# A three-stage kernel (top-k attention, a dense layer pair, routed experts): fixed engines for the weight splits of experts 2 to 7, and a new order of all operations

## The chip, the cores and the metric

One Trainium2 chip, one core of it. The metric is the device time of one execution in microseconds (us). The kernel before: median 687.64 us of 3 runs, 686.29 to 690.04.

## The reference

Three computations in a row, all in float32:

```
scores = q @ k^T / 8                      # 2 batches x 8 heads, 576 x 576, head size 64
keep the 32 largest of each row; softmax over them; attn @ v
x = attention output as 1152 tokens x 512
h = x @ w_in (512 x 2048);  x = (h * cos(h)) @ w_out (2048 x 512)
expert = argmax(x @ w_gate) of 8;  gate = its softmax weight
token t goes to slot "count so far" of its expert (capacity 288, later ones dropped)
out[t] = gate * relu(x @ w1[expert] (512 x 1024)) @ w2[expert] (1024 x 512)
```

## The kernel before, in words

**Engines.** TensorE (PE) does matmuls and transposes, VectorE (DVE), ScalarE (ACT) and GpSimd (POOL) the elementwise work, SyncE (SP) issues the loads. Each has its own queue and works through it in order.

**First stage (attention, dense pair, routing).** The 16 heads are worked in 36 steps of 128 query rows for two heads. A step: `scores` (L716, PE) and their eviction to `Sp`; `pair_chain` (L751, DVE), which finds the 32nd largest value of each row with repeated maximum and replace instructions; `softmax` (L791, ACT, POOL, DVE); `products` (L826), transposes and the product with `v`. When the steps of a tile of 128 tokens are done, `layer_in`, `cosine`, `product` and `layer_out` (L911 to L986) do the dense pair, `route` and `place` (L988, L1026) choose the expert and scatter the token rows to `xs` in DRAM. Meanwhile `convert` (L605) turns the dense weights, which arrive as 64-bit numbers, into float32.

**Expert stage.** For each of 8 experts: `gather` (L1204) loads up to 192 token rows `xg`, PE transposes them (`xp`, L1219 and L1220), ACT rounds the result into `xgs` (L1222) and DVE subtracts to get the rest (L1223). `expert_in` (L1226) multiplies with `w1` (`hp`, L1234 and L1236), ACT copies (`ht`, L1239), DVE adds (L1240), ACT applies relu and rounds (`hc`, L1241), DVE makes the rest of `hc` in two instructions (`rest`, L1244, L1247). `expert_out` (L1252) multiplies with `w2` (`yp`, L1266), ACT scales by the gate (`ot`), and POOL scatters the rows to the output (L1272). After the main path a branch handles experts with over 192 tokens.

**Weight splits.** PE multiplies a rounded part and a rest of each weight. `weights2` (L1187) loads an expert's weights in 8 pieces of 512 KB into the `raw` buffers and splits each half-piece: `rounded` (L593) makes `wh` or `wk`, on ACT (L594) or POOL (L595); `subtract` (L589) makes the rest `wl`, on DVE (L590) or POOL (L591). There are 16 of each per expert. Two sets of split weights exist, so that the splits of an expert can run while the one before it computes; a set is free again once the expert two before it has used it.

**The order.** Nothing is ordered by hand. Each operation is handed to a planner (`Plan`, L276) with an engine, a cost in us and a rank. `emit` (L340) is a list scheduler: on each engine it takes, among the operations that could start within 0.02 us of the earliest, the one with the lowest rank, and writes the instructions in that order. `RANKS` holds a rank for every operation; `flex` (L330) lets one character of `PICKS` choose the engine of an operation that can run on two or three. An operation marked `port=True` waits in the plan for the other of DVE and POOL to end its marked one (L374). `tb` is the rank penalty of an ACT operation that needs another function table than the loaded one. `PICKS` is read in program order: 9 characters for each of the 36 steps, 32 for `convert`, 140 for the dense pair, then 32 for each expert.

Of the kernel before, what the change touches and what calls it, by code (L numbers as in the profile page):

```python
# [45 lines left out]
    "0000000000000000000000000000000000000000000000001000000010000000100000000000000000000000000000000000"  # L46
    "0000000000000000000000000000000000000000000000000000000000000000000000000000000000000000000000000000"
    "0001000000000000000000000000100011001100000001122000001122000001020011000000111110000110100011000100"
    "0220000001220110011020000000000000000000001011000000000000000000000001010000000010100001000000000101"
    "0101010101000000000000001110101101010110000000101010101010101010001010111010101101011111111111110000"  # L50
    "0000000101010101000000000000001000101010010000000000000100111110001000000000010111010000000101010111"
    "0000000000010100000101010000011000010101010100000011110101010000000000000000011110101000001000101000"
    "0001010101000000000010010101010101000100000010110000")
RANKS = [
# [431 lines left out]
def forward(ctx, lasting, tc, kq, vn, vs_, w_in, w_out, w_gate, w1, w2, out, paired):  # L486
# [172 lines left out]
    def hi_of(idx):  # L659
        return ("wk" if idx[0] > 1 else "wh", (idx[0], idx[1] // 2), idx[1] % 2)  # L660
# [90 lines left out]
    def pair_chain(s):  # L751
# [8 lines left out]
        for r in range(3):  # L760
            for i in range(2):
                P.op("dve", 0.365, lambda r=r, i=i: DVE.max(T["W", s][:, i, LIST[r]:LIST[r] + 8], T["C", s][:, i, 0:HS]),  # L762
                     r=[("C", s, i)], w=[("W", s, i)])
# [629 lines left out]
```

## Time and profile before

| what | us |
|---|---|
| median of 3 runs (lowest to highest) | 687.64 (686.29 to 690.04) |
| the profiled execution | 687.24 |
| its span, first to last instruction | 685.4 |
| PE, DVE, ACT, POOL busy | 595.2, 549.7, 468.1, 345.7 |
| loads, stores | 64.57 MB, 12.69 MB |

Times in rows are us from the start of the span unless marked ns. PE is a matmul, PEld a weight load, L12 a line of the kernel. A row of the groups view reads: line, engine, operation, output<-inputs with shapes, xcount | busy us, mean ns of one | idle time of the engine just before them and who ended it. In a timeline: start, length, instruction, xcount, and in brackets the engine's idle time before it and who ended that. Matmuls are pipelined and their ends are modelled. The granted clock is a share of 2.4 GHz.

### The profile page before, as it was taken

The numbers are of one execution on the slowest core, as the hardware profiler recorded it, in microseconds if no ns is written. First come the engines' busy times: TensorE is split into PE (matmuls) and PEld (weight loads), VectorE is DVE, ScalarE is ACT, GpSimd is POOL, SyncE is SP. The second block draws the span as 40 slices with busy tenths as digits, with TensorE's granted clock in tenths as the row PEclk, the third lists the DMA queues.
The fourth block names the chain that finished last, engine by engine and source line by source line (L and its number), as shares of the span: only waits on it lengthen the run. The fifth ranks groups of instructions, "written<-read, shape, count | busy, mean of one in ns | idle before, by whom it ended". The sixth has DMA issues, their size and how long they took to land.

```text
span 685.4 us, 11005 instructions
## 1 busy us (share of the span) xinstructions
PE 595.2 (87%) x3675; PEld 440.6 (64%) x3675; DVE 549.7 (80%) x1470; ACT 468.1 (68%) x954; POOL 345.7 (50%) x396
## 2 busy tenths in 40 slices
PE   2456896999999998999999999998597977989894
PEld 1134673676866556776667767764486856978793
DVE  5999999999999998999999935664367787758860
ACT  3689799999999996886758844734255555546541
POOL 1387887566598653523646525122135546623631
PEclk9997798999999998999999999999698999999997
DMA  8553359200411111000000023443435545644710
GB/s 341 216 203 123 122 202 343 91 32 1 143 47 48 55 40 35 2 0 1 1 2 1 1 78 121 140 139 138 155 112 186 202 159 195 235 150 149 233 48 18
DMA packets 30787, 77.29 MB, mean 113 GB/s; under 512 B 4606, under 2 KB 4606, under 8 KB 30720
## 3 DMA queue, kind: packets, MB, share of 16 engines
q1 hardware_dynamic: 28976, 71.73, 30.4%
q0 software_dynamic: 1744, 4.76, 1.8%
q8 instruction: 31, 0.51, 0.3%
q14 instruction: 36, 0.29, 0.1%
HBM read 64.57 MB, written 12.69 MB: 113 GB/s over the span
## 4 chain that ended last, share of the span: by engine, by line
PE 55%; DVE 18%; ACT 15%; issue 5%; DMA 3%; POOL 2%; SPq 1%; POOLq 0%; DVEq 0%; ACTq 0%
PE x L982 15%; PE yp L1266 8%; DVE hc L1247 5%; PE h L928 4%; PE av L851 4%; PE S L729 4%; PE pt L837 4%; PE h L933 3%; PE h L934 3%; PE h L935 3%; PE hp L1234 3%; DVE C L765 2%; DVE W L762 2%; ACT pen L803 2%; ACT Sp L820 2%
## 5 line engine op out<-in xcount | busy, mean ns | idle before, releaser
L982 PE MATMUL x<-wo,hs 128*128 128x512 f32 x288 | 139.9, 609 | 1.4 <-POOL hs L972 1.3
L807 POOL TENSOR_TENSOR Sp<-Sp,pen 128x576 f32<-128x576 f32 x59 | 80.7, 1367 | 38.4 <-ACT pen L803 35.5
L765 DVE MATCH_REPLACE8 C<-W,C 128x288 f32<-128x288 f32 x216 | 94.1, 442 | 0.0
L762 DVE MAX8 W<-C 128x8 f32<-128x288 f32 x216 | 90.8, 448 | 0.6
L729 PE MATMUL S<-kq 64*128 64x288 f32 x256 | 57.4, 530 | 28.0 <-ACT Sp L599 17.6
L1234 PE MATMUL hp<-xgs,wh 128*128 128x384 f32 x256 | 78.6, 373 | 0.0
L982 PEld LDWEIGHTS x<-wo,hs 128*128 128x128 f32 x288 | 49.7, 193 | 43.3 <-issue 39.9
L1266 PE MATMUL yp<-wk,hc 128*128 128x512 f32 x192 | 71.2, 419 | 0.0
L837 PE MATMUL pt<-ident,Sp 128*128 128x128 f32 x324 | 56.0, 302 | 11.4 <-ACT Sp L820 9.9
L837 PEld LDWEIGHTS pt<-ident,Sp 128*128 128x128 f32 x324 | 40.8, 154 | 38.8 <-ACT Sp L820 17.3
L1236 PE MATMUL hp<-xgs,wl 128*128 128x192 f32 x256 | 65.6, 256 | 0.0
L757 DVE TENSOR_TENSOR C<-Sp 128x576 f32<-128x576 f32 x72 | 61.2, 851 | 4.1 <-ACT Sp L599 3.1
L803 ACT ACTIVATE pen<-Sp,tb 128x576 bf16<-128x576 f32 x72 | 55.5, 771 | 7.2 <-POOL tb L796 4.4
L810 ACT ACTIVATE Sp<-Sp,tb 128x576 f32<-128x576 f32 x72 | 55.8, 776 | 4.0 <-DVE Sp L807 2.4
L1247 DVE SCALAR_TENSOR_TENSOR hc<-ht,hc 128x128 fp32r<-128x128 f32 (+1 forms) x128 | 53.8, 476 | 5.2 <-ACT hc L1241 4.4
L729 PEld LDWEIGHTS S<-kq 64*128 64x128 f32 x256 | 22.3, 213 | 50.3 <-ACT Sp L599 31.2
L935 PE MATMUL h<-xh,wl 128*128 128x256 f32 x192 | 53.8, 280 | 0.0
L853 PE MATMUL av<-PT,v 128*64 128x128 f32 x320 | 47.8, 301 | 5.8 <-ACT PT L599 5.8
L769 DVE MAX8 W<-C 128x8 f32<-128x576 f32 x72 | 52.3, 748 | 0.2
L1266 PE MATMUL yp<-wl,hc 128*128 128x512 f32 x128 | 52.5, 410 | 0.0
L599 ACT ACTIVATE PT<-pt 128x384 f32<-128x384 f32 x97 | 44.3, 486 | 11.1 <-PE pt L837 11.1
L591 POOL TENSOR_TENSOR wl<-raw,wk 128x512 fp32r<-128x512 f32 x26 | 34.1, 1330 | 35.2 <-ACT wk L594 32.3
(158 smaller groups left out, 1572.9 us busy)
## 6 DMA issues: line engine op xcount, KB each, us to landing
raw<-in_w_dram SPq DMA_DIRECT2D x64, 512.0 KB
wraw<-in_w_in_dram SPq DMA_DIRECT2D x16, 512.0 KB
wraw<-in_w_out_dram SPq DMA_DIRECT2D x16, 512.0 KB
xs<-z SPq DMA_DIRECT2D x1, 4680.0 KB
kq<-in_kq_dram SPq DMA_DIRECT2D x8, 576.0 KB
v<-in_vn_dram SPq DMA_DIRECT2D x8, 320.0 KB
v<-in_vs_dram SPq DMA_DIRECT2D x8, 320.0 KB
out_dram<-z SPq DMA_DIRECT2D x1, 2304.0 KB
```

The source lines that it names most:

```text
L729: PE.matmul(T[kp][:, a, 0:HS], t[p, 1, j * 128:(j + 1) * 128], t[p, 0, i * HS:(i + 1) * HS], start=True, stop=True)
L762: P.op("dve", 0.365, lambda r=r, i=i: DVE.max(T["W", s][:, i, LIST[r]:LIST[r] + 8], T["C", s][:, i, 0:HS]), r=[("C", s, i)], w=[("W", s, i)])
L765: P.op("dve", 0.42, lambda r=r, i=i: DVE.match_replace(T["C", s][:, i, 0:HS], T["W", s][:, i, LIST[r]:LIST[r] + 8], T["C", s][:, i, 0:HS], ...
L803: P.op("act", 0.67, lambda i=i, kp=kp: ACT.activation(T[kp], T["Sp", s][:, i, :], AF.Relu, scale=-BIG, bias=T["tb", s][:, i, 0:1]), r=[ks, ...
L807: eng.tensor_tensor(out=T["Sp", s][:, i, :], in0=T["Sp", s][:, i, :], in1=T[kp], op=OP.subtract)
L837: PE.transpose(T[kp][:, c * 128:(c + 1) * 128], P2[:, cc * 128:(cc + 1) * 128], ident)
L935: PE.matmul(o, lo, a, start=False, stop=(kc == 3), skip_group_check=True)
L982: P.op("pe", 0.86, lambda f=f, a=a: PE.matmul(T["x2", t], T[kh][:, a:a + 128], T["wo", 0][:, f, :], start=(f == 0), stop=(f == 15)), r=[kh ...
L1234: PE.matmul(T[kp][:, 0:2 * MAIN], hi_at(ka)[:, c:c + 128], x.rearrange("p a n -> p (a n)"), start=(kc == 0), stop=False, skip_group_check= ...
L1236: PE.matmul(T[kp][:, 0:MAIN], T[kb][:, c:c + 128], x[:, 0], start=False, stop=(kc == 3), skip_group_check=True)
L1247: DVE.scalar_tensor_tensor(h[:, d:d + c1 - c0], t[:, c0:c1], 0.0, h[:, c0:c1], op0=OP.max, op1=OP.subtract)
L1266: PE.matmul(T[kp], x, w, start=(fc + n == 0), stop=(fc == 7 and n == len(uses) - 1))
```

## The change

From the third expert on (`e > 1`) the splits no longer go through `flex`: every rounding is an ACT operation and every subtraction a DVE operation with `port=True`; `PICKS` shrinks from 752 to 560 characters. `rest` gets `port=True`. A number of costs change, most of them of PE. `tb` goes from 28.19 to 41.13, and all of `RANKS` and `PICKS` are new.

```diff
 PICKS = (
-    "0000000000000000000000000000000000000000000000001000000010000000100000000000000000000000000000000000"
...
+    "0000000000000000000010000000000000000000000000001000000010000000100000100000000010000000000000000000"
...
 RANKS = [
-    13.82, 76.33, 33.9, 115.9, -5.32, -4.16, 45.32, 21.36, 15.26, -3.5, -3.67, -3.5, -3.66, -0.54, -0.54, 0, 0, 0.7,
...
+    -57.65, -11.09, -55.03, 90.68, -38.73, -35.96, -6.67, 16.37, 16.37, -2.88, -4.35, -2.88, -4.35, -0.42, -0.42,
...
-PRM = dict(... tb=28.19, ...)
+PRM = dict(... tb=41.13, ...)
...
-        P.op("pe", 0.5 if kind == "n" else 1.0, mm, r=[k], w=[kp], ...)
+        P.op("pe", 0.595 if kind == "n" else 1.025, mm, r=[k], w=[kp], ...)
...
-                P.op("dve", 0.365, lambda r=r, i=i: DVE.max(T["W", s]...
+                P.op("dve", 0.372, lambda r=r, i=i: DVE.max(T["W", s]...
...
-        P.op("pool", 0.3, scalars, r=both + [("halfpi",)], w=[("edge", s), ("tb", s)])
+        P.op("pool", 0.5, scalars, r=both + [("halfpi",)], w=[("edge", s), ("tb", s)])
...
-            P.op("pe", 0.33, tr, r=parts + [CONST], w=[kp], duty=0.5)
+            P.op("pe", 0.345, tr, r=parts + [CONST], w=[kp], duty=0.5)
...
-        P.op("pe", 1.12 if kind == "n" else 2.2, av, ...
+        P.op("pe", 1.16 if kind == "n" else 2.24, av, ...
...
-                P.op("pe", 0.86, mm, r=xs_ + [("ws", w) for w in ws], w=[kp])
+                P.op("pe", 0.9, mm, r=xs_ + [("ws", w) for w in ws], w=[kp])
...
-                P.op("pe", 1.43, mm, r=xs_ + ...
+                P.op("pe", 1.46, mm, r=xs_ + ...
...
-            P.op("pe", 0.86, lambda f=f, a=a: PE.matmul(T["x2", t], ...
+            P.op("pe", 0.87, lambda f=f, a=a: PE.matmul(T["x2", t], ...
...
+    def T_part(k, a):
+        return lambda: T[k][:, a * 512:(a + 1) * 512]
+
     def weights2(e, i):
...
         for a in range(2):
             hi, lo = wkey("wh", e, i, a), wkey("wl", e, i, a)
-            rounded(lambda a=a, hi=hi: (hi_at(hi), T[kr][:, a * 512:(a + 1) * 512]), r=[kr], w=[hi])
-            subtract(lambda a=a, hi=hi, lo=lo: dict(out=T[lo], in0=T[kr][:, a * 512:(a + 1) * 512], in1=hi_at(hi)),
-                     r=[kr, hi], w=[lo])
+            part = T_part(kr, a)
+            if e > 1:
+                P.op("act", 0.52, lambda hi=hi, part=part: ACT.activation(hi_at(hi), part(), AF.Copy), r=[kr], w=[hi])
+                P.op("dve", 0.6, lambda hi=hi, lo=lo, part=part: DVE.tensor_tensor(
+                    out=T[lo], in0=part(), in1=hi_at(hi), op=OP.subtract), r=[kr, hi], w=[lo], port=True)
+                continue
+            rounded(lambda hi=hi, part=part: (hi_at(hi), part()), r=[kr], w=[hi])
+            subtract(lambda hi=hi, lo=lo, part=part: dict(out=T[lo], in0=part(), in1=hi_at(hi)), r=[kr, hi], w=[lo])
...
-        P.op("dve", 0.33, rest, r=[kt], w=[kc_])
+        P.op("dve", 0.335, rest, r=[kt], w=[kc_], port=True)
```

What the two strings of `PICKS` choose, counted by the operations in program order (number of operations on each engine, before and after):

| operation | before | after |
|---|---|---|
| scores evicted to `Sp`, steps 0 to 35 | ACT 67, DVE 5 | ACT 60, DVE 12 |
| penalty subtracted in `softmax` (L807) | POOL 59, DVE 13 | POOL 52, DVE 20 |
| scaling in `softmax` (L820 to L822) | ACT 59, DVE 3, POOL 10 | ACT 59, DVE 9, POOL 4 |
| transposes evicted to `PT` | ACT 97, DVE 11 | ACT 86, DVE 22 |
| `convert`, first operation | ACT 29, POOL 3 | ACT 26, POOL 6 |
| `layer_in`: eviction; clamp | ACT 15, DVE 21; POOL 23, DVE 13 | ACT 21, DVE 15; POOL 34, DVE 2 |
| `product` | POOL 23, DVE 13 | POOL 29, DVE 7 |
| `split_w`: rounding; subtraction | ACT 16; DVE 9, POOL 7 | ACT 14, POOL 2; DVE 6, POOL 10 |
| experts 0 and 1: rounding; subtraction | ACT 27, POOL 5; DVE 24, POOL 8 | ACT 19, POOL 13; DVE 18, POOL 14 |
| experts 2 to 7: rounding; subtraction | ACT 78, POOL 18; DVE 56, POOL 40 | ACT 96; DVE 96 (fixed) |

Nearly all of the changed picks of the steps lie in steps 19 to 35.

## Rows read from the trace of the kernel before

**Rows 1.** Windows: stretch, length; busy PE, PEld, DVE, ACT, POOL; clock; DMA share, GB/s
```profile
60.00:76.90 16.90, 12.12 (x64) 8.42 (x66) 16.57 (x46) 14.76 (x28) 14.52 (x14) 0.50 0.46 154
...
107.70:114.40 6.70, 5.94 (x14) 3.07 (x15) 6.53 (x12) 6.67 (x12) 6.70 (x7) 0.50 1.03 349
...
114.40:257.80 143.40, 139.44 (x980) 93.53 (x980) 138.83 (x410) 138.94 (x280) 94.28 (x110) 1.00 0.19 66
...
257.80:264.60 6.80, 6.06 (x35) 3.81 (x34) 5.45 (x20) 2.90 (x7) 2.03 (x4) 0.50 0.10 39
...
264.60:476.00 211.40, 209.37 (x1331) 146.39 (x1330) 164.09 (x455) 140.56 (x251) 85.75 (x115) 1.00 0.15 51
...
490.80:675.30 184.50, 164.82 (x890) 146.65 (x888) 131.25 (x292) 94.74 (x252) 81.59 (x73) 0.94 0.48 161
```

**Rows 2.** PE's waits after 500 us, and two in its timeline
```profile
PE xp L1219 <- DVE xgs L1223: 19.5, 7, 4.7
...
555.43 0.47 PE L1219 MATMUL xp<-ident,xg 128*128 128x128 f32 x1 [4.66 <-DVE xgs L1223]
...
622.49 0.33 PE L1219 MATMUL xp<-ident,xg 128*128 128x128 f32 x1 [1.60 <-DVE xgs L1223]
```

**Rows 3.** DVE and POOL timelines around one hole, and two undisturbed DVE rows
```profile
544.11 4.33 DVE L1247 SCALAR_TENSOR_TENSOR hc<-ht,hc 128x128 fp32r<-128x128 f32 x2
...
544.34 3.81 POOL L591 TENSOR_TENSOR wl<-raw,wk 128x512 fp32r<-128x512 f32 x3
...
526.97 0.77 DVE L1247 SCALAR_TENSOR_TENSOR hc<-ht,hc 128x128 fp32r<-128x128 f32 x4
...
505.81 0.68 DVE L590 TENSOR_TENSOR wl<-raw,wh 128x512 fp32r<-128x512 f32 x1
```

**Rows 4.** POOL timeline: last split before the experts, and the next
```profile
470.65 1.29 POOL L591 TENSOR_TENSOR wl<-raw,wk 128x512 fp32r<-128x512 f32 x1
...
501.82 1.82 POOL L595 TENSOR_SCALAR wh<-raw 128x512 fp32r<-128x512 f32 x3 [18.58 <-PE hp L1234]
```

**Rows 5.** Windows at the low clock after five of the holes
```profile
526.33:530.91 4.58, 4.58 (x17) 4.39 (x18) 3.25 (x14) 1.78 (x6) 0.00 (x0) 0.50 0.29 110
...
sum 17.60, PE 17.59 PEld 15.14 DVE 11.58 ACT 9.77 POOL 4.86; mean PE 3.52 PEld 3.03 DVE 2.32 ACT 1.95 POOL 0.97
```

**Rows 6.** Groups of DVE by shape, 500 to 676 us
```profile
L1247 DVE SCALAR_TENSOR_TENSOR hc<-ht,hc 128x128 fp32r<-128x128 f32 x61 | 33.8, 554 | 4.8 <-ACT hc L1241 4.0 <-ACT wk L594 0.4
...
L1247 DVE SCALAR_TENSOR_TENSOR hc<-ht,hc 128x64 fp32r<-128x64 f32 x62 | 25.9, 417 | 0.0
...
L590 DVE TENSOR_TENSOR wl<-raw,wh 128x512 fp32r<-128x512 f32 x30 | 23.9, 832 | 3.2 <-POOL wh L595 2.1 <-ACT wh L594 1.2
...
L590 DVE TENSOR_TENSOR wl<-raw,wk 128x512 fp32r<-128x512 f32 x26 | 22.8, 900 | 4.1 <-ACT wk L594 4.0
```

**Rows 7.** Groups of POOL and ACT by shape, 500 to 676 us
```profile
L591 POOL TENSOR_TENSOR wl<-raw,wk 128x512 fp32r<-128x512 f32 x22 | 29.0, 1339 | 23.9 <-ACT wk L594 21.1 <-PE xp L1219 2.4 <-issue 0.2
...
L591 POOL TENSOR_TENSOR wl<-raw,wh 128x512 fp32r<-128x512 f32 x18 | 24.7, 1387 | 17.7 <-ACT wh L594 17.5
...
L595 POOL TENSOR_SCALAR wh<-raw 128x512 fp32r<-128x512 f32 x9 | 7.2, 813 | 25.2 <-PE hp L1234 18.6 <-DMA raw<-in_w_dram 6.6
...
L595 POOL TENSOR_SCALAR wk<-raw 128x512 fp32r<-128x512 f32 x9 | 6.3, 699 | 4.3 <-DMA raw<-in_w_dram 4.3
...
L594 ACT ACTIVATE wk<-raw 128x512 fp32r<-128x512 f32 x39 | 23.1, 622 | 5.3 <-DMA raw<-in_w_dram 3.2 <-PE yp L1266 2.1
```

**Rows 8.** Groups of DVE, whole span: work of the first stage
```profile
L600 DVE TENSOR_SCALAR Sp<-S 128x576 f32<-128x576 f32 x5 | 3.8, 753 | 0.2
...
L600 DVE TENSOR_SCALAR PT<-pt 128x384 f32<-128x384 f32 x11 | 6.0, 550 | 2.6 <-PE pt L837 2.6
...
L807 DVE TENSOR_TENSOR Sp<-Sp,pen 128x576 f32<-128x576 f32 x13 | 9.8, 752 | 0.1
...
L821 DVE TENSOR_SCALAR Sp<-Sp,sm 128x576 f32<-128x576 f32 x3 | 1.5, 514 | 0.0
```

More of the change, by code (lines that the diff above doesn't have):

```diff
@@ L45 @@
 PICKS = (
-    "0000000000000000000000000000000000000000000000001000000010000000100000000000000000000000000000000000"
[L47 to L53, printed above, removed]
-RANKS = [
[212 rows of a table removed]
+    "0000000000000000000010000000000000000000000000001000000010000000100000100000000010000000000000000000"
+    "0000000000000000000000000000000000000000000000000000000000000000000000010000000010000000000000000000"
+    "0001000000020000000111011010111111101112001000111000001120000001100001001100011101100111001100111110"
+    "0000011100021101111100111111000000000000000011000000000000000000000000001010000010100011000000000101"
+    "0101010101010000111100001010101000100000110000000000000000100000000011110000101110100000000000101101"
+    "010100000010000001000001000100000010101010101011111111010111")
+RANKS = [
[220 rows of a table added]
 ]
-PRM = dict(np=10, cl=16, ts=0, na=32, mul=3, c0=-6.12, c1=-0.119, c2=-35.561, c3=2.753, sm=-13.198, pr=-0.47, sc=3.501, mx=-2.942, co=16.076, lo=16.671, ro=8.401, tb=28.19, ga=7.38, lod=16, pc=8, lv=15.338, sw=11.123, s1=2.383, pick=PICKS, ranks=RANKS)
+PRM = dict(np=10, cl=16, ts=0, na=32, mul=3, c0=-6.12, c1=-0.119, c2=-35.561, c3=2.753, sm=-13.198, pr=-0.47, sc=3.501, mx=-2.942, co=16.076, lo=16.671, ro=8.401, tb=41.13, ga=7.38, lod=16, pc=8, lv=15.338, sw=11.123, s1=2.383, pick=PICKS, ranks=RANKS)
 FULL = dict(np=4, cl=2, ts=0, na=12, mul=8, c0=3.627, c1=-2.562, c2=3.854, c3=0.425, sm=1.002, pr=3.858, sc=5.283, mx=0.736, co=8.685, lo=1.174, ro=7.507, tb=11.194, ga=4.52, lod=4, pc=0, lv=2.808, sw=1.416, s1=0.894)
@@ L741, in copy @@
             return o, T[kp][:, :, 0:HS]
-        P.op("pe", 0.5 if kind == "n" else 1.0, mm, r=[k], w=[kp], tiling="rows" if kind == "n" else "quarters")
+        P.op("pe", 0.595 if kind == "n" else 1.025, mm, r=[k], w=[kp], tiling="rows" if kind == "n" else "quarters")
         evict(0.53, 0.67, copy, r=[kp], w=[("Sp", s, i)], scale=0.125)
@@ L761, in pair_chain @@
             for i in range(2):
-                P.op("dve", 0.365, lambda r=r, i=i: DVE.max(T["W", s][:, i, LIST[r]:LIST[r] + 8], T["C", s][:, i, 0:HS]),
+                P.op("dve", 0.372, lambda r=r, i=i: DVE.max(T["W", s][:, i, LIST[r]:LIST[r] + 8], T["C", s][:, i, 0:HS]),
                      r=[("C", s, i)], w=[("W", s, i)])
@@ L867, in products @@
             vs = [ka, kc]
-        P.op("pe", 1.12 if kind == "n" else 2.2, av, r=[("PT", (s, g)) for g in range(3)] + vs, w=[ko],
+        P.op("pe", 1.16 if kind == "n" else 2.24, av, r=[("PT", (s, g)) for g in range(3)] + vs, w=[ko],
              tiling="columns" if kind == "n" else None)
@@ L936, in layer_in @@
             if one:
-                P.op("pe", 0.86, mm, r=xs_ + [("ws", w) for w in ws], w=[kp])
+                P.op("pe", 0.9, mm, r=xs_ + [("ws", w) for w in ws], w=[kp])
             else:
-                P.op("pe", 1.43, mm, r=xs_ + [k for w in ws for k in (hi_of(w), ("wl", w))], w=[kp])
+                P.op("pe", 1.46, mm, r=xs_ + [k for w in ws for k in (hi_of(w), ("wl", w))], w=[kp])
         evict(0.48, 0.6, lambda: (T[kh], T[kp]), r=[kp], w=[kh])
@@ L981, in layer_out @@
             f, a = n * u + c, c * (512 // n) + z * 128
-            P.op("pe", 0.86, lambda f=f, a=a: PE.matmul(T["x2", t], T[kh][:, a:a + 128], T["wo", 0][:, f, :], start=(f == 0),
+            P.op("pe", 0.87, lambda f=f, a=a: PE.matmul(T["x2", t], T[kh][:, a:a + 128], T["wo", 0][:, f, :], start=(f == 0),
                                                         stop=(f == 15)),
```

430 rows, old and new, of the table RANKS are left out of this document.

## The prediction, made before the changed kernel was run

> **What bounds the kernel now.** I read the windows by stage first. Up to 257.8 us VectorE (DVE) is the full engine (138.83 of 143.4 us); from 264.6 to 476 it is TensorE (PE), 209.37 of 211.4 us at the full clock; in the expert stage, 490.8 to 675.3, nobody is: PE 164.82 of 184.5, DVE 131.25, ScalarE (ACT) 94.74, GpSimd (POOL) 81.59 [rows 1]. So the expert stage loses time in waits, and PE's waits there were read next. After 500 us PE waits for one thing: seven times, 19.5 us in all, the transposes of the next expert's tokens (`xp`, L1219) wait for DVE's `xgs` subtraction (L1223) that frees their PSUM buffer; the longest takes 4.66 us [rows 2].
>
> Why is DVE late? The two timelines side by side tell it. At 544.11 two `hc` instructions (L1247) take 4.33 us, and POOL runs three weight subtractions from 544.34 for 3.81 us; four of the same DVE instructions take 0.77 us at 526.97, when POOL does nothing [rows 3]. A DVE instruction with two SBUF inputs stands still while POOL's tensor work runs. All of that POOL work belongs to experts 2 to 7: the last split of experts 0 and 1 on POOL is at 470.65, the next one, at 501.82, waited for expert 0 to release its weights [rows 4], and the counts after 500 us (22+18 subtractions, 9+9 roundings [rows 7]) are those that the old pick string gives to POOL from the third expert on.
>
> Each hole is paid twice. After five of the seven the granted clock stands at 0.50, that is 1.2 of 2.4 GHz; the stretches of it in which PE works sum to 17.60 us [rows 5], so half of that, 8.8 us, is lost. A hole of 1.60 us [rows 2] is not among the five.
>
> **The change, part by part.** The sum goes against the profiled execution, 687.24 us (span 685.4; the median of the three runs, 687.64, is 0.4 above).
>
> *Splits of experts 2 to 7.* 40 subtractions and 18 roundings leave POOL. DVE gets 40 x 0.68 us, the undisturbed length [rows 3], = +27.2 us. It loses its stalls: `hc` shows 33.8+25.9 = 59.7 us for 61.5 pairs [rows 6] that cost 0.77/2 = 0.385 us undisturbed [rows 3], so 23.7, a stall of 36.0; its own 56 subtractions show 23.9+22.8 = 46.7 us [rows 6] against 56 x 0.68 = 38.1, a stall of 8.6. Together -44.6. DVE's stage goes from 131.25 to about 113.9 us: it takes on 40 instructions and still gets lighter.
> Here a rule is to be weighed. The Trainium skill, Perfetto Trace Analysis, section Optimizing Scalar/DVE Operations, says that elementwise work may be handed to Scalar or even GPSIMD where DVE is saturated, and adds that between GPSIMD and DVE this might not help because they share a port; by its first half the change would cost DVE its 27.2 us and give nothing, by its second half it would give the stall back, and the sum above is the second.
> ACT gets 18 x 0.622 = 11.2 us [rows 7] on 94.74 of 184.5 [rows 1]: 106 us, hidden as long as the stage is longer than that.
>
> *What the stage can reach.* 184.5 - 19.5 - 8.8 = 156.2 us, 19.5 per expert. All seven holes were behind POOL, so all can go. Two things are charged against that. First, DVE's and ACT's queues run in a fixed order, and a subtraction in front of an urgent `xgs` can still make PE wait: between no hole (0) and all seven (28.3). I take one in seven, 28.3/7 = 4, nearer to none because DVE's 113.9 us fill 73% of 156.2. Second, POOL's roundings waited 6.6+4.3 = 10.9 us for weight loads [rows 7]; on ACT such a wait holds up the copies of PE's results (`ht`, `hc`, `xgs`) queued behind it, and PE behind these. Ends 0 and 10.9; I take 2, since ACT idles a third of the time even at 156 us. The loads on SP's queue now wait for DVE alone to free a `raw` buffer, with the gathers of `xg` queued behind; no hole ends at a transfer today [rows 2], and DVE frees a buffer 0.68 us after ACT's rounding where POOL took 1.3 us [rows 7], so 0. Expert stage: -28.3 + 4 + 2 = **-22.3 us**.
>
> *`rest` marked as sharing the port, L1247.* Costs nothing itself: it makes the planner keep POOL's remaining tensor work (experts 0 and 1) off the `hc` instructions.
>
> *More POOL work for experts 0 and 1.* 14 subtractions and 13 roundings instead of 8 and 5. Before, they were over at 470.65 [rows 4], beside PE's full stretch [rows 1]; 14 more pieces of 0.7 to 1.3 us [rows 7] find room there, 0. If they slip past 500 us, the first hole (of seven) comes back; that is inside the 4.
>
> *The first stage in a new order.* The planner's PE costs rise by about 14 us in all (64 x 0.095 for scores, 48 x 0.04 and 48 x 0.03 for `layer_in`, 108 x 0.015 for transposes, 144 x 0.01 for `layer_out`, 36 x 0.04 for the product with `v`), so the old order was made for a PE that is too fast. The trace shows no such order, so it is bounded: the low clock in the first stage covers 16.9+6.7+6.8 us with PE busy in 12.12+5.94+6.06 = 24.1 of them [rows 1], worth 12 us at most if the new order avoids it; the loss end is a later DVE (rival 3), taken as +10. The picks move ACT's evictions of late steps to DVE: 7 x 0.753 + 11 x 0.550 + 6 x 0.514 + 7 x 0.752 (the last from POOL) = 19.7 us [rows 8], while 26 pieces of the dense pair leave DVE for POOL or ACT. The picks of steps 0 to 18 hardly change, and where DVE is full [rows 1] no order makes it less so. I take -3, what the low clock at 257.8 alone costs (6.06/2), the one break between the DVE-bound and the PE-bound stretch.
> Table loads: `tb` rises, so fewer switches between `exp` and `sin` are wanted; ACT is not what PE waits for after 264.6 [rows 1], 0.
>
> *Sum.* 687.2 - 22.3 - 3 = **662 us**, 3.7% below.
>
> **The rivals.**
> 1. *DVE stays late half of the time.* The splits stand in front of `xgs` in DVE's order at three or four of seven boundaries. For: the order is fixed before the run, and all 16 subtractions of an expert now pass one queue. Against: 73% load. Half of 28.3 stays: 687.2 - 14.2 + 2 - 3 = 672.
> 2. *VectorE is the scarce engine after all.* The 27.2 us added to DVE come back on the path and eat the gain of 28.3. For: 40 instructions of 0.68 us really are added to it. Against: the stall that leaves is larger (44.6). 687.2 - 28.3 + 27.2 + 2 - 3 = 685, about no change. This is what the skill's first half-rule would make of it; the traces speak against it.
> 3. *Slower.* In the last third of attention (about 250 to 390 us) DVE takes the 19.7 us of evictions and becomes the bound where PE is full today [rows 1, 8]; PE waits for scores and probabilities, and the clock falls as in the earlier stretches, 12 us more. 687.2 - 22.3 + 19.7 + 12 = 697. It decides from the point where DVE's share in 264 to 390 reaches the whole and PE's falls below 90%. Against: DVE has 211.4 - 164.09 = 47 us free there [rows 1].
> 4. *The first stage gains for real.* The low clock goes: 687.2 - 22.3 - 12 = 653.
> 5. *The change does not do what it says:* POOL still has work past 500 us from experts 0 and 1, and the first two or three holes stay. 28.3 x 3/7 = 12 stays instead of the 4 charged: 670, beside rival 1.
>
> **How the numbers follow.** Forecast 0.58; rivals 1 and 5 together 0.16; rival 2 0.05; rival 3 0.09; rival 4 0.12. A measurement of this kernel tells about 0.5%, 3.4 us, from no change. Faster: 0.58+0.16+0.12 = 0.86; same 0.05; slower 0.09. The range: the forecast's own is 656 to 669 (holes between none and two, -4 to +4; loads between 0 and 5, -2 to +3); 650 to 680 takes in rivals 1, 4 and 5 and leaves out 2 and 3 and the tails, a little under 0.2.
>
> **What would show it.** Right: no L590, L591 or L595 work of POOL after about 500 us but the 16 scatters; `hc` at 0.2 to 0.3 us everywhere; subtractions at 0.68, 96 of them on DVE for experts 2 to 7; PE's wait for `xgs` under 5 us instead of 19.5; the expert stage at 160 to 166 us with the clock near 1.00. Wrong: holes before L1219 of 2 us and more with POOL idle (rival 1 or 2), ACT's roundings waiting for loads for over 5 us with PE idle behind them, or a first stage that ends more than 5 us away from 490.8 (rivals 3 and 4).

## The result, and the profile after

The changed kernel takes 656.18 us (median of 4 runs, 655.3 to 656.63), the kernel before, on the same chip, 688.15. The ratio is 0.953 (95% interval 0.951 to 0.956). The profiled execution took 656.63 us against 687.24, so 30.6 us are to be found between the two traces. Ratios here compare fast executions only; the one median below with slow executions in it is that of "the mark alone" (2 of its 10, at 693.1).

The windows by stage of the changed kernel come first (stretch, length; busy PE, PEld, DVE, ACT, POOL with their instructions; granted clock; DMA share, GB/s). The expert stage now runs from 489.8 to 645.8.

```profile
114.40:257.80 143.40, 137.55 (x965) 92.44 (x961) 139.22 (x399) 133.32 (x266) 97.98 (x117) 0.99 0.19 59
264.60:476.00 211.40, 207.02 (x1314) 143.08 (x1310) 163.78 (x450) 132.08 (x233) 91.18 (x125) 1.00 0.13 43
489.80:645.80 156.00, 155.91 (x890) 140.38 (x888) 114.42 (x332) 104.85 (x270) 14.95 (x15) 0.99 0.58 196
```

The third row answers to the last one of [rows 1]. TensorE is busy for 155.91 of 156.0 us, and the waits view of 500 to 646 us has no row for it: the seven holes of [rows 2] are gone, and with them the low clock of [rows 5]. The stage lasts 156.0 us instead of 184.5, which is 28.5 of the 30.6. The first stage ends 1.0 us earlier (489.8 against 490.8), and the end after the last `yp` is 1.1 us shorter (9.0 against 10.1). The two other rows moved little: VectorE fills the first as before and has as much free in the second as a whole.

The groups of the expert stage by shape tell what became of the splits, first those of DVE (busy us, mean ns of one | idle time before, and who ended it):

```profile
L1212 DVE TENSOR_TENSOR wl<-raw,wk 128x512 fp32r<-128x512 f32 x48 | 31.7, 684 | 3.1 <-ACT wk L1211 2.7
L1212 DVE TENSOR_TENSOR wl<-raw,wh 128x512 fp32r<-128x512 f32 x48 | 31.1, 685 | 4.4 <-ACT wh L1211 4.2
L1254 DVE TENSOR_TENSOR ht<-hp,ht 128x192 f32<-128x192 f32 x64 | 21.3, 351 | 10.0 <-ACT ht L1253 9.3 <-ACT wh L1211 0.4
L1261 DVE SCALAR_TENSOR_TENSOR hc<-ht,hc 128x128 fp32r<-128x128 f32 x64 | 18.2, 285 | 3.2 <-ACT hc L1255 2.5 <-issue 0.4
L1261 DVE SCALAR_TENSOR_TENSOR hc<-ht,hc 128x64 fp32r<-128x64 f32 x64 | 13.9, 218 | 0.0
```

the splits' share of ACT in the same view:

```profile
L1211 ACT ACTIVATE wk<-raw 128x512 fp32r<-128x512 f32 x48 | 28.5, 627 | 1.4 <-DMA raw<-in_w_dram 1.1
L1211 ACT ACTIVATE wh<-raw 128x512 fp32r<-128x512 f32 x48 | 27.8, 623 | 6.2 <-DMA raw<-in_w_dram 6.0 <-PE hp L1248 0.2
```

and, from the profile page, whose groups take in the whole span, what POOL does there:

```profile
L1286 POOL DMA_INDIRECT out_dram<-ot,ti x16 | 15.9, 991 | 143.9 <-ACT ot L1295 114.6
```

All 96 subtractions are on DVE at 0.68 us; the 56 that DVE had in [rows 6] took 0.83 and 0.90. The two `hc` instructions take 285 and 218 ns where they took 554 and 417. ACT waits 6.0+1.1 = 7.1 us for weight loads, and no hole of PE follows. Of POOL's 16 scatters 15 fall in the stage (the x15 of the window above), and they are all that POOL does in it.

The chain that ended last says the same from the other side. First the kernel before, then the one after (shares of the span by engine, then by line):

```profile
PE 55%; DVE 18%; ACT 15%; issue 5%; DMA 3%; POOL 2%; SPq 1%; POOLq 0%; DVEq 0%; ACTq 0%
PE x L982 15%; PE yp L1266 8%; DVE hc L1247 5%; PE h L928 4%; PE av L851 4%; PE S L729 4%; PE pt L837 4%; PE h L933 3%; PE h L934 3%; PE h L935 3%; PE hp L1234 3%; DVE C L765 2%; DVE W L762 2%; ACT pen L803 2%; ACT Sp L820 2%
```

```profile
PE 47%; DVE 34%; ACT 9%; issue 4%; DMA 3%; POOL 2%; SPq 0%; POOLq 0%; DVEq 0%; ACTq 0%
PE yp L1280 11%; PE x L988 8%; PE hp L1248 8%; DVE C L771 8%; DVE W L768 7%; DVE C L763 6%; DVE W L775 4%; PE hp L1250 4%; PE S L735 3%; PE h L939 2%; PE pt L843 2%; DVE wt L649 2%; PE h L940 2%; PE h L941 2%; PE av L857 2%
```

Before, `DVE hc L1247` held 5% of the span on the chain; after, no expert-stage line of DVE is in the list, and the three expert matmuls (`yp`, `hp`, `hp`) hold 11+8+4%. DVE's whole share rose to 34% all the same, through `C` and `W`: the part of the first stage that VectorE bounds. A chain's shares say where it runs, not what got slower.

### The profile page after: what moved, and what is told of

The parts are those of the page before. It is cut to its first block, busy times and chain, and to the rows that moved or that the text cites. A ratio compares the mean times of both kernels' runs of the same rounds, so it can differ in the third digit from the quotient of the medians.

```text
span 654.8 us, 10920 instructions
## 1 busy us (share of the span) xinstructions
PE 581.5 (89%) x3675; PEld 430.8 (66%) x3675; DVE 535.6 (82%) x1509; ACT 464.7 (71%) x947; POOL 291.8 (45%) x364
## 4 chain that ended last, share of the span: by engine, by line
PE 47%; DVE 34%; ACT 9%; issue 4%; DMA 3%; POOL 2%; SPq 0%; POOLq 0%; DVEq 0%; ACTq 0%
PE yp L1280 11%; PE x L988 8%; PE hp L1248 8%; DVE C L771 8%; DVE W L768 7%; DVE C L763 6%; DVE W L775 4%; PE hp L1250 4%; PE S L735 3%; PE h L939 2%; PE pt L843 2%; DVE wt L649 2%; PE h L940 2%; PE h L941 2%; PE av L857 2%
## 5 line engine op out<-in xcount | busy, mean ns | idle before, releaser
L988 PE MATMUL x<-wo,hs 128*128 128x512 f32 x288 | 138.0, 601 | 1.5 <-POOL hs L978 1.5
L813 POOL TENSOR_TENSOR Sp<-Sp,pen 128x576 f32<-128x576 f32 x52 | 70.3, 1352 | 41.1 <-ACT pen L809 40.8
L735 PE MATMUL S<-kq 64*128 64x288 f32 x256 | 55.3, 512 | 28.0 <-ACT Sp L605 17.3
L1286 POOL DMA_INDIRECT out_dram<-ot,ti x16 | 15.9, 991 | 143.9 <-ACT ot L1295 114.6
L843 PEld LDWEIGHTS pt<-ident,Sp 128*128 128x128 f32 x324 | 38.9, 151 | 47.8 <-ACT Sp L826 26.6
L1280 PE MATMUL yp<-wk,hc 128*128 128x512 f32 x192 | 67.5, 398 | 0.0
L826 ACT ACTIVATE Sp<-Sp,sm 128x576 f32<-128x576 f32 x59 | 43.1, 777 | 15.1 <-DVE sm L821 15.1
L934 PE MATMUL h<-xn,ws 128*128 128x128 f32 x384 | 50.5, 283 | 2.1 <-ACT hs L605 1.7
L775 DVE MAX8 W<-C 128x8 f32<-128x576 f32 x72 | 51.9, 745 | 0.2
L934 PEld LDWEIGHTS h<-xn,ws 128*128 128x128 f32 x384 | 46.6, 196 | 7.0 <-ACT hs L605 3.6
L1280 PE MATMUL yp<-wl,hc 128*128 128x512 f32 x128 | 50.3, 393 | 0.0
```

Source lines behind the costliest of these rows:

```text
L735: PE.matmul(T[kp][:, a, 0:HS], t[p, 1, j * 128:(j + 1) * 128], t[p, 0, i * HS:(i + 1) * HS], start=True, stop=True)
L775: P.op("dve", 0.665, lambda i=i: DVE.max(T["W", s][:, i, 40:48], T["C", s][:, i, :]), r=[("C", s, i), ("C", s, 2)], w=[("W", s, i)])
L813: eng.tensor_tensor(out=T["Sp", s][:, i, :], in0=T["Sp", s][:, i, :], in1=T[kp], op=OP.subtract)
L843: PE.transpose(T[kp][:, c * 128:(c + 1) * 128], P2[:, cc * 128:(cc + 1) * 128], ident)
L934: PE.matmul(o, T["ws", w][:, cols], T["xn", t][:, kc], start=(kc == 0), stop=(kc == 3), skip_group_check=True)
L988: P.op("pe", 0.87, lambda f=f, a=a: PE.matmul(T["x2", t], T[kh][:, a:a + 128], T["wo", 0][:, f, :], start=(f == 0), stop=(f == 15)), r=[kh ...
```

## The experiments

In the texts on record "theory" is mine at that time. A stage time below is from the first `hp` to the last `yp` of the run's profiled execution; lines in rows are those of the kernel that ran.

### The engines without the order, and the plan without the engines

**Old order, other engines.** The kernel before, with its own order of all operations; the 58 splits of experts 2 to 7 that stand on POOL are issued at the same places by ACT and DVE.

```diff
-    ("pool", 1.27, lambda: POOL.tensor_tensor(op=OP.subtract, **args()), True)
+    ("pool", 1.27, lambda: (DVE if fixed else POOL).tensor_tensor(op=OP.subtract, **args()), True)
...
-    ("pool", 0.59, lambda: POOL.tensor_scalar(*args(), 1.0, 0.0, op0=OP.mult, op1=OP.add), True)
+    ("pool", 0.59, lambda: ACT.activation(*args(), AF.Copy) if fixed else
+     POOL.tensor_scalar(*args(), 1.0, 0.0, op0=OP.mult, op1=OP.add), True)
```

> The kernel before with its own order of all operations, its own costs and ranks; only the instructions of the 58 weight splits of experts 2 to 7 that POOL did are issued on ACT (18 roundings) and DVE (40 subtractions) at the same place of the order. Theory (POOL's tensor work held DVE still, and PE's transposes waited for DVE): the seven holes go although the order is the old one; the expert stage falls from 184.5 us to 156 to 166, the whole to 657 to 669 us. Rival (the new order, planned with the port in mind, brought the gain): without it most holes stay, the expert stage is over 172 us and the whole over 675 us.

**Old ranks, new plan.** The kernel before with the `e > 1` branch of the diff, and nothing else of it: old ranks, old picks for the rest, old costs, no mark on `rest`. The planner knows the engines and orders anew.

> The kernel before with the fixed engines from the third expert on, planned again with the old ranks, picks and costs, and without the port mark on the rest of hc. Theory: as in the run before, 657 to 669 us, and within 5 us of it, since POOL is out of the expert stage either way. Rival (order): over 672 us.

**The mark alone.** The kernel before with `port=True` on `rest`, ordered anew; POOL keeps its splits.

```diff
-        P.op("dve", 0.33, rest, r=[kt], w=[kc_])
+        P.op("dve", 0.335, rest, r=[kt], w=[kc_], port=True)
```

> The kernel before with the rest of hc marked as sharing the port (cost 0.335, port=True) and nothing else: POOL keeps its 58 splits, the planner now keeps them off the hc instructions. Theory (POOL in the expert stage is what costs): the stalls become planned waits, DVE and PE are late as before or a little less; 675 to 690 us. Rival (the planner only had to know): at least half of the 28 us comes back, 660 to 673 us.

| kernel | median us | ratio to before (95%) | stage | PE's holes over 0.25 us in it |
|---|---|---|---|---|
| old order, other engines | 663.44 | 0.965 (0.961 to 0.970) | 162.1 | 4.2 |
| old ranks, new plan | 657.48 | 0.957 (0.953 to 0.961) | 156.7 | none |
| the mark alone | 688.46 | 1.000 (0.997 to 1.003) | 185.9 | 23.4 |

The waits of PE from 500 us on, in the old order with the other engines (us in total, times, longest):

```profile
PE xp L1219 <- DVE xgs L1223: 4.2, 6, 1.3
```

Holes before the same instruction as in [rows 2], but six and 4.2 us instead of seven and 19.5, and behind none of them does the clock fall. So the change of engine alone, without any new order, gives 24 of the 32 us, and what is left of the holes is the price of an order that was made for POOL. A new plan by the old ranks takes 6 more (the text on record had the two within 5 of each other). New ranks, costs and the mark are worth 1.3 together. The intervals of the ratios overlap, though the executions of the two kernels do not (656.81 to 657.64 against 655.3 to 656.63); they were not run side by side, so whether this is a difference stays open. The effect of the corrected costs by themselves was not tried.

The mark alone gives nothing. Its two longest waits of PE:

```profile
PE xp L1219 <- DVE xgs L1223: 12.7, 4, 4.8
PE hp L1236 <- POOL wl L591: 9.1, 3, 5.8
```

and rows of its POOL and DVE timelines (start, length, instruction, count):

```profile
639.03 4.74 POOL L591 TENSOR_TENSOR wl<-raw,wh 128x512 fp32r<-128x512 f32 x1
639.56 1.28 DVE L590 TENSOR_TENSOR wl<-raw,wk 128x512 fp32r<-128x512 f32 x2
640.77 0.68 DVE L590 TENSOR_TENSOR wl<-raw,wh 128x512 fp32r<-128x512 f32 x1
641.37 1.29 DVE L590 TENSOR_TENSOR wl<-raw,wk 128x512 fp32r<-128x512 f32 x2
```

Some holes went, and a new kind came: PE waits for a subtraction that POOL makes. At 639.03 one of these takes 4.74 us instead of 1.3 [rows 7], while DVE runs five of its own back to back at their undisturbed 0.68. This time POOL stands still. The plan moved a part of the stall to the other engine; the rest stayed, for `hc` still takes 24.6+27.3 = 51.9 us in this stage, against 59.7 in [rows 6].

### POOL's work given back, one kind at a time

After's own order; the splits that POOL had before (40 subtractions, 18 roundings) are issued by POOL again, first both, then each kind alone. `OLD` is the old pick string of experts 2 to 7.

```diff
+                n = 32 * (e - 2) + 4 * i + 2 * a
-                P.op("act", 0.52, lambda hi=hi, part=part: ACT.activation(hi_at(hi), part(), AF.Copy), r=[kr], w=[hi])
+                P.op("act", 0.52, lambda hi=hi, part=part, n=n: (
+                    POOL.tensor_scalar(hi_at(hi), part(), 1.0, 0.0, op0=OP.mult, op1=OP.add) if OLD[n] == "1" else
+                    ACT.activation(hi_at(hi), part(), AF.Copy)), r=[kr], w=[hi])
-                P.op("dve", 0.6, lambda hi=hi, lo=lo, part=part: DVE.tensor_tensor(
+                P.op("dve", 0.6, lambda hi=hi, lo=lo, part=part, n=n: (POOL if OLD[n + 1] == "1" else DVE).tensor_tensor(
```

> The changed kernel with its own order, only that 40 subtractions and 18 roundings of experts 2 to 7 (those of the old pick string) are issued on POOL at the place where ACT and DVE had them. Theory: hc instructions stand still for 1.3 us a piece again, holes before the xp transposes come back, the clock falls after them: 672 to 692 us, expert stage 172 to 190. Rival (order): the new order carries it, within 6 us of 656.

> As the run that put POOL back into the changed kernel, but only the 40 subtractions (two SBUF inputs on POOL, 1.3 us each); the 18 roundings stay on ACT. Theory: any tensor instruction of POOL holds a DVE instruction with two SBUF inputs for its whole length, so most of the 18 us comes back, 667 to 676 us. Rival (it is the roundings, which on POOL wait for loads and hold up its queue): 656 to 662.

> Only the 18 roundings are issued on POOL (one SBUF input, 0.65 us each); all subtractions stay on DVE. Theory: POOL's tensor work is then 12 of 69 us, and pieces of 0.65 us are too short to make a hole: 656 to 661 us. Rival (the roundings): 665 us and more.

| on POOL again | median us | ratio to before (95%) | stage |
|---|---|---|---|
| both kinds | 674.13 | 0.983 (0.978 to 0.988) | 174.6 |
| 40 subtractions | 672.03 | 0.978 (0.975 to 0.981) | 173.8 |
| 18 roundings | 658.76 | 0.959 (0.957 to 0.962) | 159.5 |

The run with the subtractions, its expert stage as one window:

```profile
488.20:662.00 173.80, 163.32 (x890) 145.13 (x888) 116.92 (x292) 104.30 (x269) 70.47 (x55) 0.96 0.52 177
```

its longest waits of PE:

```profile
PE xp L1238 <- DVE xgs L1242: 5.4, 3, 3.2
PE xp L1238 <- DMA xg<-xs: 2.4, 1, 2.4
```

and three of its DVE groups:

```profile
L1266 DVE SCALAR_TENSOR_TENSOR hc<-ht,hc 128x128 fp32r<-128x128 f32 x64 | 26.4, 413 | 5.4 <-ACT hc L1260 4.7 <-issue 0.4
L1266 DVE SCALAR_TENSOR_TENSOR hc<-ht,hc 128x64 fp32r<-128x64 f32 x64 | 21.5, 335 | 0.0
L1259 DVE TENSOR_TENSOR ht<-hp,ht 128x192 f32<-128x192 f32 x64 | 21.0, 349 | 13.7 <-ACT ht L1258 12.8 <-issue 0.6
```

In the run with the roundings the `hc` groups read:

```profile
L1266 DVE SCALAR_TENSOR_TENSOR hc<-ht,hc 128x128 fp32r<-128x128 f32 x64 | 20.0, 312 | 3.0 <-ACT hc L1260 2.3 <-issue 0.4
L1266 DVE SCALAR_TENSOR_TENSOR hc<-ht,hc 128x64 fp32r<-128x64 f32 x64 | 14.2, 222 | 0.0
```

The subtractions are the cost: 15.9 us of 18.0 (672.03 and 674.13 against 656.18); the roundings cost 2.6. With the subtractions on POOL the two `hc` groups take 47.9 us instead of 32.1, while `ht`, with one of its two inputs in PSUM, stays at 349 ns. That agrees with the Trainium skill (SBUF — State Buffer, Who interferes with whom), by which a DVE instruction with two SBUF inputs contends with a GpSimd instruction that reads SBUF, and one with at most one such input does not, outside the 2-port performance modes. One input alone does not protect an instruction in this case: `ti`, a cast with one SBUF input, takes 0.16 us in the mean in after, but in the kernel before, beside a subtraction that POOL starts at 551.22:

```profile
551.37 1.16 DVE L1214 CAST ti<-xg 128x2 int32<-128x2 f32 x1
```

Whether such a mode is the reason, no run here shows.

With the subtractions on POOL, DVE's sum hardly differs, 116.92 us against 114.42, though it has 40 instructions fewer; the stage is 17.8 us longer. What costs is that the lost time comes in pieces of up to 2.8 us (the longest `hc`; in after 0.29) ahead of what PE waits for, with three stretches at the low clock behind.

Together with the old order above this gives four corners (medians):

| | splits partly on POOL | on ACT and DVE |
|---|---|---|
| order of before | 687.6 | 663.4 |
| order of after | 674.1 | 656.2 |

The engines are worth 18 to 24 us, the order 7 to 13.5, and each is worth more without the other: both shorten the same holes. The order's part has the new first stage in it (1 to 2.6 us, see the section on the prediction).

### How much room VectorE has

My prediction leaned on DVE being busy for only 73% of the new stage. Three kernels load it further. In after's order, `rest` issues each of its two instructions twice, with the same values; then a plan that is told of the doubled cost (on "old ranks, new plan", `rest` at 0.67); then, in after's order, only the shorter of the two twice.

```diff
-                DVE.scalar_tensor_tensor(h[:, d:d + c1 - c0], t[:, c0:c1], 0.0, h[:, c0:c1], op0=OP.max, op1=OP.subtract)
+                for _ in range(2):
+                    DVE.scalar_tensor_tensor(h[:, d:d + c1 - c0], t[:, c0:c1], 0.0, h[:, c0:c1], op0=OP.max,
+                                             op1=OP.subtract)
...
+                for _ in range(2 if c0 else 1):
```

> The changed kernel with its own order; each of the two instructions of the rest of hc is issued twice (same values), 128 more DVE instructions of 0.2 to 0.3 us, some 25 us more of DVE in the expert stage (114 of 156 us before). Theory (DVE has room once POOL is out): the time rises by less than 8 us. Rival (DVE is the scarce engine and the changed kernel sits just under its bound): it rises by 15 to 25 us.

> The run with fixed engines and the old ranks (657.5 us), with the rest of hc issued twice as in the run before, but told to the planner (cost 0.67 instead of 0.33), so that the order is made for it. Theory (the 23 us of the run before came from an order that did not know of the extra work; DVE itself, 146 us of 156, still has room): 660 to 669 us. Rival (with 146 us and its waits for ACT, DVE is the bound, whatever the order): 673 us and more.

> The changed kernel with its own order; only the narrower of the two instructions of the rest of hc (128x64) is issued twice, 64 more DVE instructions, 13.9 us by the groups (some 9 us where they follow each other), where both together, 25 to 33 us, cost 23 us. A threshold (DVE's spare time absorbs the first of it): 656 to 660 us. In proportion (every us of DVE in the expert stage lies on the path, so the changed kernel is already bound by DVE and TensorE together): 664 to 670 us.

| kernel | median us | ratio to before (95%) | DVE in the stage | stage |
|---|---|---|---|---|
| after | 656.18 | 0.953 | 114.4 | 156.0 |
| shorter one twice | 665.5 | 0.970 (0.966 to 0.973) | 127.8 | 163.7 |
| both twice | 679.37 | 0.991 (0.987 to 0.994) | 145.9 | 180.3 |
| both twice, planned for | 679.5 | 0.988 (0.985 to 0.991) | 146.7 | 179.5 |

The theory that the doubled `rest` would hide fell: 23 us more, and a plan that knows of it gets no better (22 above its own base of 657.48). That does not clear the order, for not all of this plan's loss is the wait for `xgs` (7.0 us in six holes). One hole is another:

```profile
PE hp L1243 <- ACT wh L1205: 5.8, 1, 5.8
```

PE waits here for the rounding of an expert's weights on ACT, and ACT for the load, while DVE is idle for part of the time; behind it the clock stands at 0.50 for 6.9 us, half of which is lost. Without this hole the run would be at some 670 us (an estimate: 679.5 - 5.8 - 3.4), just above the theory's 669 and below the rival's 673, so it decides for neither. The half dose shows no cliff: 13.4 us more of DVE lengthen the stage by 7.7, 31.5 us by 24.3. (The profiled execution of the half dose took 663.1 us, the shortest of its four.)

The mean hides why. Windows of after, the start, the middle and the end of the expert stage, and two 10-us pieces of the middle:

```profile
490.00:515.00 25.00, 25.00 (x143) 23.21 (x143) 14.07 (x42) 15.55 (x40) 1.94 (x2) 0.94 0.57 186
515.00:525.00 10.00, 9.98 (x62) 8.95 (x61) 9.99 (x36) 8.01 (x26) 0.00 (x0) 1.00 0.48 168
...
600.00:610.00 10.00, 10.00 (x65) 9.59 (x65) 10.00 (x31) 8.48 (x22) 0.00 (x0) 1.00 0.67 227
515.00:625.00 110.00, 109.97 (x633) 98.66 (x632) 90.41 (x256) 79.83 (x205) 10.12 (x10) 1.00 0.68 227
625.00:645.80 20.80, 20.73 (x117) 18.31 (x115) 9.94 (x34) 9.47 (x28) 2.88 (x3) 1.00 0.11 41
```

DVE is at 56% in the first 25 us and 48% in the last 21; in the 110 us between it is at 82%, and for 10 us at a time at 100%. There it has nothing to spare. The half dose shows what happens. Of its 163.7 us PE is idle for 4.9 (after: 0.1 of 156.0) and busy for 2.9 more. Its longest wait:

```profile
PE xp L1233 <- DVE xgs L1237: 4.2, 6, 1.0
```

and DVE and PE in its timeline at the longest of these holes (in brackets the idle time before, and who ended it):

```profile
541.28 0.68 DVE L1262 SCALAR_TENSOR_TENSOR hc<-ht,hc 128x128 fp32r<-128x128 f32 x3
541.94 0.17 DVE L1228 CAST ti<-xg 128x2 int32<-128x2 f32 x1
542.02 0.35 DVE L1254 TENSOR_TENSOR ht<-hp,ht 128x192 f32<-128x192 f32 x1
542.29 0.68 DVE L1212 TENSOR_TENSOR wl<-raw,wk 128x512 fp32r<-128x512 f32 x1
...
542.89 0.35 DVE L1237 TENSOR_TENSOR xgs<-xp,xgs 128x192 fp32r<-128x192 f32 x1
...
543.29 0.33 PE L1233 MATMUL xp<-ident,xg 128*128 128x128 f32 x1 [0.99 <-DVE xgs L1237]
```

DVE works without a gap, every instruction at its undisturbed length, POOL is idle, and a subtraction (542.29) stands ahead of the `xgs` (542.89) that PE waits for. That is rival 1's picture, but in one of the six holes only. In the other five it is `hc` that stands ahead, as in the second longest (0.89 us, ending at 521.51):

```profile
520.24 0.68 DVE L1262 SCALAR_TENSOR_TENSOR hc<-ht,hc 128x128 fp32r<-128x128 f32 x3
520.84 0.35 DVE L1254 TENSOR_TENSOR ht<-hp,ht 128x192 f32<-128x192 f32 x1
521.11 0.35 DVE L1237 TENSOR_TENSOR xgs<-xp,xgs 128x192 fp32r<-128x192 f32 x1
```

So the doubled instruction stands in the urgent chain itself. The three runs show that DVE has no room there; whether the same 13 us at a less urgent place, in the first 25 us of the stage for instance, would hide, was not tried.

### Two edits that changed nothing

**PE kept busy before the first expert.** In after, PE waits 6.6 us for the first expert's rows, and its first 3.2 us of `hp` run at the low clock. 26 matmuls of the identity fill the wait.

```diff
+                for _ in range(26 if e == 0 and c == 0 else 0):
+                    PE.matmul(T[kp][:, 256:384], ident, ident, start=True, stop=True, skip_group_check=True)
```

> The changed kernel with 26 extra 128x128 float32 matmuls of the identity, whose results nobody reads, issued while PE waits 6.6 us for the first expert's token rows (480 to 487 us). Theory of the clock (PE's rest there is what brings it to 1.2 GHz until 493): the clock stays at 1.00 and the first products take 9.6 us, not 11.8, so 1 to 2.5 us less. Rival (the products wait for the xgs chain, not for the clock): no change, within 0.7 us; the extra matmuls end later than the rows arrive: 0.5 to 2 us more.

It took 655.87 us (655.3 to 657.5; ratio 0.956, 0.954 to 0.959), no difference from after. The windows of this run:

```profile
476.00:483.10 7.10, 5.09 (x45) 4.77 (x44) 2.90 (x22) 1.02 (x3) 5.37 (x6) 0.52 0.52 189
483.10:489.00 5.90, 5.18 (x46) 4.88 (x46) 1.11 (x3) 0.55 (x2) 4.58 (x5) 1.00 0.76 238
...
488.90:500.20 11.30, 10.87 (x75) 10.27 (x75) 6.01 (x23) 6.00 (x19) 0.00 (x0) 1.00 0.43 160
```

and of after:

```profile
476.00:489.80 13.80, 4.63 (x44) 3.55 (x44) 4.43 (x25) 1.67 (x6) 10.91 (x11) 0.63 0.64 221
489.80:493.00 3.20, 3.20 (x14) 3.20 (x13) 0.62 (x2) 0.55 (x2) 0.00 (x0) 0.50 0.96 332
493.00:501.60 8.60, 8.60 (x63) 8.58 (x62) 5.39 (x21) 5.50 (x17) 0.00 (x0) 0.99 0.21 79
```

The edit does what it should: the clock is at 1.00 (2.4 GHz) when the first `hp` starts. But that block gets only 0.5 us shorter (11.3 against 3.2+8.6 = 11.8), and PE, which had no gap in it, now idles 11.30-10.87 = 0.43 us. Half of the 3.2 us, 1.6, was there to be won by the clock (the text on record had 2.2, 11.8 less 9.6); 0.5 arrived, and 0.43 us of the rest is PE's new idle time. What holds the remainder was not settled.

**Experts 0 and 1 too.** In after's order, the 27 splits of experts 0 and 1 on POOL are issued by ACT and DVE as well.

> The changed kernel with its own order; the 13 roundings and 14 subtractions of experts 0 and 1 that POOL still does are issued on ACT and DVE at the same place. Theory (they run beside TensorE's full stretch and before the first expert, and cost nothing): 655 to 658 us. Rival (POOL holds DVE there too, in front of the first expert's tokens): 650 to 654 us; or DVE and ACT get late in the dense pair: 658 us and more.

It took 655.74 us (655.64 to 658.86; ratio 0.955, 0.953 to 0.958): the same as after. POOL's work for the first two experts costs nothing that these runs can tell.

## Why the prediction was right, and where its steps were off

The time, 656.2, lies inside the range and inside the forecast's own 656 to 669, at its lower end; the direction and the mechanism were right, and the sum (-25.3) was 5.3 us short of the measured -30.6. The steps missed by more than the sum: the stage by 6.2, and the first stage by 2.0 the other way. By its steps:

- **The floor of the stage (156.2).** Measured 156.0, below the 160 to 166 named as a sign of being right. Both parts of the 28.3 us, holes and low clock, came back whole. But "all seven holes were behind POOL" was more than the trace says. Beside the hole that ends at 602.35 POOL does nothing from 599.31 on:

```profile
602.35 0.33 PE L1219 MATMUL xp<-ident,xg 128*128 128x128 f32 x1 [2.45 <-DVE xgs L1223]
598.67 0.64 POOL L595 TENSOR_SCALAR wk<-raw 128x512 fp32r<-128x512 f32 x1 [1.18 <-DMA raw<-in_w_dram]
603.54 1.20 POOL L595 TENSOR_SCALAR wh<-raw 128x512 fp32r<-128x512 f32 x2 [4.23 <-DMA raw<-in_w_dram]
```

  Nor does it beside the one that ends at 622.49 [rows 2]: POOL is idle there from 618.34 to 625.79. What made DVE late there is not shown. With the old order and the new engines six holes are left, so the new plan was needed too.
- **DVE's stall (44.6).** Mis-sized. DVE's 113.9 us were 114.42 and ACT's 106 were 104.85, and the subtractions have the undisturbed 0.68. But the step took `hc`'s 59.7 us from the groups view, which adds up overlapping instructions, and its undisturbed 0.385 us a pair from a timeline of four in a row. In the groups view an undisturbed pair takes 285+218 = 503 ns: the stall of `hc` was 59.7 - 61.5 x 0.503 = 28.8 us, and with the subtractions' 8.6 some 37, still more than the 27.2 that came. That DVE's stage came out as forecast does not prove these terms: 131.25 - 37 + 27 would be 121, for the window counts overlapping instructions once and the groups twice.
- **The charges (+4 for DVE's order, +2 for ACT's loads).** Mis-sized: both are 0 in the changed kernel, and they are the stage's 6.2 us. The 4 is the price of the old order: with it and the new engines the stage is 162.1, 5.9 above the floor, 4.2 of it in six holes before `xp`. I charged an order that the change throws away. The 2 was found in neither order: from 500 us on PE has no wait for ACT over 0.2 us in either. In the changed kernel ACT's wait for loads did come (7.1 us, where I named over 5 as a sign of trouble) and nothing of PE's stood behind it.
- **The room on DVE (73%).** The number was right and the reading wrong. I took it for room, against rivals 1 and 2; the half dose shows that 13 us more, on `hc`, put six holes back. Rival 2 was refuted because the stall that leaves is larger than the work that comes, as its "against" says, not because DVE had time to spare.
- **The first stage (-3).** Measured -1.0 in the profiled executions. The low clock at 257.8 went, as I took it, but others came. In after the low clock stands here (windows by stretch):

```profile
42.68:49.50 6.82, 5.04 (x27) 3.55 (x29) 6.63 (x18) 5.83 (x11) 4.24 (x4) 0.50 0.51 158
52.92:63.10 10.18, 6.42 (x35) 4.13 (x35) 10.15 (x29) 9.25 (x20) 7.55 (x8) 0.50 0.54 192
66.58:76.80 10.22, 4.82 (x28) 3.68 (x29) 10.22 (x29) 7.42 (x16) 8.79 (x10) 0.50 0.30 104
148.50:151.90 3.40, 3.40 (x16) 3.40 (x17) 3.40 (x13) 2.43 (x6) 3.09 (x3) 0.50 0.00 0
```

  That is 30.6 us of it against 30.4 in [rows 1]; it moved to where DVE is full anyway. But the profiled execution is the slowest of its four. Five other kernels above do the same first stage in the same order (POOL's work given back, three times, and the two with a doubled `rest` in after's order); none of them has the last of these stretches, and their first `hp` starts at 488.2 to 488.5, 2.3 to 2.6 us before the 490.8 of the kernel before (491.1 in the old order with the new engines). The -3 was nearer than one trace says. What part of it the corrected durations of PE gave was not tried.
- **The mark on `rest`, and POOL's work for experts 0 and 1 (0 each).** Nothing speaks against either: the mark gave nothing in the old kernel and was not taken out of the changed one alone; POOL's work was moved in the changed kernel, without a difference.
- **What the sum left out.** The end after the last `yp`, 1.1 us shorter.

The difference of 5.3 us is then 6.2 (the stage, 28.5 against 22.3) less 2.0 (the first stage) plus 1.1 (the end).

Of the rivals, 1 and 2 name the limit that the changed kernel sits just under; 3 came half: in its own window, 264 to 390 us, DVE did fill up (124.78 of 126.0 us, 118.65 before; the 47 us that spoke against it lie later), but PE stayed busy for 123.22 of them (124.19 before) and the clock at 1.00. 4 and 5 did not come. What stays open is how much of the 1.3 us between "old ranks, new plan" and after is real, and which of its parts gives it.

## What to carry to other kernels

Where an engine's instructions come in two lengths, look at what POOL does beside the long ones before counting loads: moving work onto the busier engine shortened this stage, because the stalls that POOL caused were larger than the work that came (some 37 us against 27) and came in lumps ahead of the urgent instruction. Read an engine's room from windows of some 10 us, not from the mean of a stage, and test it by issuing a cheap instruction twice, knowing that this tests the place where the instruction stands. Here the old order cost 6 us with engines that it was not made for: charge such a price only if the old order stays.

## What was not expected of the hardware

The conflict between DVE and POOL has no fixed loser. In the kernel before, DVE stood still through POOL's subtractions, 4.33 us for two `hc` instructions beside three of POOL's [rows 3], 4.19 of them for one; with the mark alone, one POOL subtraction took 4.74 us beside five of DVE's. In both cases the one that stands still waits through several instructions of the other, not one.

Most of what POOL's work costs goes with its time, some with its kind. In after's order, 40 subtractions (55.0 us of POOL by their groups, `hc` 15.8 us longer) cost 15.9 us of the whole; 18 roundings (13.4 us of POOL, `hc` 2.1 us longer) cost 2.6. That is 4.1 times the time and 6.1 times the cost: 0.29 us for each us of POOL's subtractions, 0.19 for each of its roundings.
